# Attention, two mixtures and a router on one core: column maxima of k by halves, and the first batch's subtraction as matmuls into PSUM

## The chip, the cores and the metric

One NeuronCore of one Trainium2 chip runs the whole program. The engines are TensorE (PE; its weight loads are shown as PEld), VectorE (DVE), ScalarE (ACT), GpSimd (POOL) and SyncE (SP), which issues the DMAs here. Each engine runs its own list of instructions in order and waits on semaphores. The metric is the device time of one execution in microseconds; lower is better.

## The reference, cut to what matters

```python
q_s = exp(q - max(q, axis=-1));  q_s = q_s / (sum(q_s, axis=-1) + 1e-9)
k_s = exp(k - max(k, axis=2));   k_s = k_s / (sum(k_s, axis=2) + 1e-9)   # over the sequence
kv  = einsum('bhsd,bhse->bhde', k_s, v)
x   = einsum('bhsd,bhde->bhse', q_s, kv)      # 4 batches, 8 heads, 576 rows, 64 columns
x   = reshape(transpose(x), (2304, 512))
h   = maximum(x @ w_in, 0);  g = s * h * h + b;  x2 = g @ w_out          # 512 -> 2048 -> 512
out = one of 8 experts for each row of x2 (router, capacity 576)          # 512 -> 1024 -> 512
```

The maximum of k is taken for each batch, head and column over the 576 rows of the sequence, subtracted, and exponentiated. All inputs are float32.

## The kernel before

The program has four parts that overlap: linear attention, the dense layer (`h_unit`, `x2_unit`), the router, and the experts. Tokens go in nine groups of 256. Attention works by batch and by pair of heads: for batch b and pair j, `load_k` and `load_v` bring k and v, and a chain follows.

- `k_max` (L352) takes the maximum over the rows that lie in one partition, with one VectorE reduce. Batch 0 holds 96 partitions of 6 rows and both heads (96x768 in, 96x128 out), the other batches 128 partitions of 5 rows. Its result is in one of two buffers (tag `rt`).
- `k_T` (L359) transposes that on TensorE, `k_cm` (L366) reduces the transposed block on VectorE to one column `cm` (two buffers in pool `sm`).
- `k_bc` (L372) makes a matmul of `cm`, broadcast, with the identity, so that each partition has the maxima in a PSUM bank; `k_sub` (L377) subtracts it from k in place on VectorE, or on GpSimd after a copy by ScalarE for the pairs in `PAR["kpool"]`; `k_exp` (L388) is one ScalarE exponential in place.
- `k_kv` (L397) multiplies with v and a column of ones, `k_rec` and `k_blk` divide and write the block `kvb`.

For q there are `q_max`, `q_sub` (GpSimd), `q_exp`, `q_sum`, `q_norm` (GpSimd), the transposes `q_T`, `q_Te`, then `x1_mm` with `kvb`, and `x1_hi`, `x1_lo`, which split x into two parts (tiles x1h and x1l). Groups 0 and 1 come first, both of batch 0.

The weights of the dense layer arrive as 32 blocks of 512 KB and are converted by `cv_abs` (ScalarE), `cv_low`, `cv_sign`, `cv_join` (VectorE), `cv_hi` (ScalarE) and `cv_lo` (VectorE). `cv_sign` (L202) is done by VectorE for the blocks in `PAR["bv"]`, else by ScalarE. Sixteen-bit views (`half`) pick the sign bits.

A dense unit is 24 matmuls (L548 to L550) of a block of 256 tokens, one for each product of parts; it needs x1h and x1l of its group and the converted weight blocks. The first unit therefore waits for the whole chain of batch 0. Before it, `warm` matmuls on the identity fill gaps that the planner expects on TensorE.

What sets the order: every step has a slot, a shift in `PAR["d"]` (with `_0` for the early steps) is added, and `arrange` (L1503) places the steps engine by engine with a table of durations, of buffers and of dependences in `parts`. The engines then run exactly that order. The banks of batch 0's chain come from the four buffers `x2` of pool `ps_x`. `parts` doesn't list the buffers of `cm`.

Of the kernel before, what the change touches and what calls it, by code (L numbers as in the profile page):

```python
# [23 lines left out]


@with_exitstack
def kernel(ctx, tc, q, k, v, w_in, w_out, s_in, b_in, w_gate, w1, w2, cap, out, dbg=None):
    nc = tc.nc
    B, H, S, D = q.shape
# [4 lines left out]
    P = 128  # L34
# [6 lines left out]
    KR = S // P  # L41
# [104 lines left out]
    def at_slot(s, f, *a):  # L146
        plan.setdefault(s, []).append((f, a))
# [203 lines left out]

    def k_max(b, j):  # L352
        t = kt[b, j]
        p = P if b else P0
        m = at.tile([P, 2, D], F32, tag="rt", name="m1", bufs=2)
        nc.vector.tensor_reduce(out=m[:p], in_=t[:p].rearrange("p h r d -> p h d r"), axis=AX.X, op=ALU.max)
        kx[b, j] = m[:p]

    def k_T(b, j):  # L359
        m2 = kx[b, j]  # L360
        ps = aux(b, [P, P], "psk")
        p = m2.shape[0]
        nc.tensor.transpose(ps[:, :p], m2.rearrange("p h d -> p (h d)"), ident[:p, :p])
# [914 lines left out]
    def parts(f, a):  # L1278
# [18 lines left out]
        elif f in (k_max, k_T, k_cm, k_bc, k_sub, k_exp, k_kv, k_rec, k_blk):  # L1297
            k = b, j = a
            bank, kt_, vt_ = ("x2", f"wi{12 + j}", f"wo{12 + j}") if b == 0 else ("a", "k", "v")
            work, after, takes, gives = {  # L1300
                k_max: ([("DVE", 0.75 if b else 0.85)], [(load_k, *k)], ["rt"], []),
                k_T: ([("PE", 0.12)], [(k_max, *k)], [bank], [((k_max, *k), "rt")]),
                k_cm: ([("DVE", 0.29)], [(k_T, *k)], [], [((k_T, *k), bank)]),
                k_bc: ([("PE", 0.25)], [(k_cm, *k)], [bank], []),
                k_sub: (
                    [("ACT", 0.28), ("POOL", 1.75)] if k in PAR["kpool"] else [("DVE", 0.81 if b else 0.93)],
                    [(k_bc, *k)], ["bc"] if k in PAR["kpool"] else [], [((k_bc, *k), bank), (key, "bc")],
                ),
                k_exp: ([("ACT", 0.74 if b else 0.87)], [(k_sub, *k)], [], []),
                k_kv: (  # L1310
                    [("PE", 0.88 if b else 1.6)], [(k_exp, *k), (load_v, *k)], [bank], [((load_k, *k), kt_), ((load_v, *k), vt_)]
                ),
# [37 lines left out]
        elif f in (cv_abs, cv_low, cv_sign, cv_join, cv_hi, cv_lo):  # L1350
# [391 lines left out]
```

## Time and profile before

| | us |
|---|---|
| median of three runs | 562.85 (561.86 to 563.61) |
| the profiled execution, whole | 563.43 |
| its span, first to last instruction | 561.7 |
| TensorE busy | 536.7 (96%) |
| VectorE busy | 329.9 (59%) |
| ScalarE busy | 234.8 (42%) |
| GpSimd busy | 141.3 (25%) |

Times in the views are in us from the start of the span. A table by stage gives, for each stretch, its length and the busy time of PE, PEld, DVE, ACT and POOL with the number of instructions, then the granted clock of TensorE as a share of full speed, the mean busy share of the DMA engines and GB/s. A timeline row gives start, length, engine, line, operation, output and input tiles, and in brackets the idle time before it with what ended it; xN merges N instructions that follow each other, and a float32 matmul shows as two records. A row by form gives the count, the busy time in all and the mean in ns of one, then the idle time before the group. Line numbers are those of the kernel before. "SPq" is the queue that SyncE issues DMAs to.

### The profile page before, as it was taken

The page shows a single profiled execution, that of the slowest core. Times are in us where ns is not written, and L with a number is a line of the kernel's source. Part 1 is how long each engine was busy: PE and PEld are TensorE (multiplying, and loading weights), DVE is VectorE, ACT ScalarE, POOL GpSimd, SP SyncE. Part 2 cuts the span into 40 slices and gives each one's busy share as a digit, 9 for nine tenths or more (in the row PEclk, how much of TensorE's full clock was granted, in tenths as well). Part 3 has the DMA queues.
Part 4 walks back from the last instruction along what each step waited for, and adds up shares of the span by engine and source line. Part 5 has one row for each costly group of instructions (what it writes and reads, how often), then busy time and mean ns, then how long its engine had stood idle before and what let it go on. Part 6 is the DMA issues. An engine that isn't in the chain of part 4 may idle for free. (4 is left out here: it accounts for less than half of the span.)

```text
span 561.7 us, 10739 instructions
## 1 busy us (share of the span) xinstructions
PE 536.7 (96%) x4087; PEld 482.0 (86%) x4087; DVE 329.9 (59%) x743; ACT 234.8 (42%) x425; POOL 141.3 (25%) x198
## 2 busy tenths in 40 slices
PE   8889999999999999999999999999999899999993
PEld 7779998988988888999998899999888887899762
DVE  5999899996596678452646145473633576073010
ACT  2688868854533434332323323222342345162110
POOL 4240012212465455211131033320014116210111
PEclk9999999999999999999999999999999999999998
DMA  8988901044541322010010201006737029523000
GB/s 238 380 265 301 371 1 46 2 126 115 157 132 46 83 69 81 1 39 20 20 39 1 57 2 25 17 2 189 227 97 222 13 58 376 169 78 113 39 25 29
DMA packets 83332, 59.96 MB, mean 107 GB/s; under 512 B 40191, under 2 KB 75647, under 8 KB 83264
## 3 DMA queue, kind: packets, MB, share of 16 engines
q1 hardware_dynamic: 81104, 54.08, 31.7%
q0 software_dynamic: 2160, 5.01, 2.7%
q8 instruction: 39, 0.64, 0.5%
q14 instruction: 29, 0.24, 0.1%
HBM read 46.64 MB, written 12.51 MB: 105 GB/s over the span
## 5 line engine op out<-in xcount | busy, mean ns | idle before, releaser
L548 PE MATMUL psh<-x1h,wi 128*128 128x256 f32 x576 | 169.1, 294 | 1.3 <-PEq L652 0.4
L549 PE MATMUL psh<-x1l,wi 128*128 128x256 f32 x576 | 163.7, 284 | 1.5 <-DVE x1l L526 1.5
L550 PE MATMUL psh<-x1h,wi 128*128 128x256 f32 x576 | 163.6, 284 | 0.0
L548 PEld LDWEIGHTS psh<-x1h,wi 128*128 128x128 f32 x576 | 111.1, 193 | 5.7 <-issue 3.6
L549 PEld LDWEIGHTS psh<-x1l,wi 128*128 128x128 f32 x576 | 111.0, 193 | 2.6 <-DVE x1l L526 1.8
L550 PEld LDWEIGHTS psh<-x1h,wi 128*128 128x128 f32 x576 | 110.8, 192 | 0.0
L570 ACT ACTIVATE rt<-psh 128x512 f32<-128x512 f32 x44 | 26.3, 598 | 67.1 <-PE psh L550 63.5
L578 DVE SCALAR_TENSOR_TENSOR rt<-rt,sb_s 128x512 f32<-128x512 f32 x44 | 38.0, 863 | 26.8 <-ACT rt L570 26.6
L614 PE MATMUL psx<-wo,gh 128*128 128x512 f32 x128 | 51.8, 405 | 0.0
L615 PE MATMUL psx<-wo,gh 128*128 128x512 f32 x128 | 50.1, 391 | 0.0
L616 PE MATMUL psx<-wo,gl 128*128 128x512 f32 x128 | 50.0, 390 | 0.0
L570 ACT ACTIVATE rg<-psh 128x512 f32<-128x512 f32 x28 | 16.5, 597 | 60.4 <-PE psh L550 45.4
L578 DVE SCALAR_TENSOR_TENSOR rg<-rg,sb_s 128x512 f32<-128x512 f32 x28 | 21.9, 786 | 28.1 <-ACT rg L570 28.0
L473 POOL TENSOR_TENSOR qt<-qt,qm 128x512 f32<-128x512 f32 x14 | 16.6, 1204 | 80.5 <-DVE qm L465 68.0
L252 POOL TENSOR_TENSOR wS<-wo 128x128 f32<-128x128 f32 x64 | 32.1, 532 | 17.1 <-DVE wT L259 15.7
L600 DVE SCALAR_TENSOR_TENSOR gl<-rt,sb_b,gh 128x512 fp32r<-128x512 f32 x32 | 28.2, 884 | 5.6 <-ACT gh L591 5.6
L386 POOL TENSOR_TENSOR kt<-kt,bc 128x640 f32<-128x640 f32 (+1 forms) x8 | 14.9, 1858 | 59.5 <-ACT bc L382 59.5
L616 PEld LDWEIGHTS psx<-wo,gl 128*128 128x128 f32 x128 | 24.0, 188 | 5.3
L614 PEld LDWEIGHTS psx<-wo,gh 128*128 128x128 f32 x128 | 24.3, 190 | 4.8 <-issue 0.6
L964 POOL DMA_INDIRECT out<-y,mp x11 | 10.6, 965 | 70.1 <-ACT y L963 52.9
L491 POOL TENSOR_TENSOR qt<-qt,qs 128x1024 f32<-128x1024 f32 x7 | 14.7, 2103 | 53.6 <-DVE qs L486 53.0
L591 ACT ACTIVATE gh<-rt,sb_b 128x512 fp32r<-128x512 f32 x32 | 23.0, 718 | 12.1 <-DVE rt L578 12.0
(228 smaller groups left out, 1134.1 us busy)
## 6 DMA issues: line engine op xcount, KB each, us to landing
ri<-in_moe_w_in SPq DMA_DIRECT2D x16, 512.0 KB, 6.3
ro<-in_moe_w_out SPq DMA_DIRECT2D x16, 512.0 KB, 8.7
raw<-in_moe_w SPq DMA_DIRECT2D x12, 512.0 KB, 5.8
raw<-in_moe_w SPq DMA_DIRECT2D x24, 256.0 KB, 5.7
out<-zero SPq DMA_DIRECT2D x9, 512.0 KB, 6.7
kt<-in_k SPq DMA_DIRECT2D x12, 256.0 KB, 2.8
vt<-in_v SPq DMA_DIRECT2D x24, 128.0 KB, 3.0
x2d<-zero SPq DMA_DIRECT2D x5, 512.0 KB
```

The lines of the kernel that those rows point to most:

```text
L252: nc.gpsimd.tensor_tensor(t[:, c], hi, lo, ALU.add)
L473: nc.gpsimd.tensor_tensor(qt[n][:, :, r], t[:, :, r], qx[n][:, :, r:r + 1].to_broadcast([P, H, D]), ALU.subtract)
L548: nc.tensor.matmul(ps, wt[:, 0, o], xh[:, c % 2], start=(c == 0), stop=False)
L549: nc.tensor.matmul(ps, wt[:, 0, o], xl[:, c % 2], start=False, stop=False)
L550: nc.tensor.matmul(ps, wt[:, 1, o], xh[:, c % 2], start=False, stop=(c == NC - 1))
L570: nc.scalar.activation(t, ps, AF.Relu)
L578: nc.vector.scalar_tensor_tensor(t, t, sb_s, t, op0=ALU.mult, op1=ALU.mult)
L591: nc.scalar.activation(gh, t, AF.Identity, bias=sb_b)
L600: nc.vector.scalar_tensor_tensor(gl, t, sb_b, gh.bitcast(F32), op0=ALU.add, op1=ALU.subtract)
L614: nc.tensor.matmul(ps, gh[:, i, o], wt[:, 0], start=(f == 0), stop=False)
L615: nc.tensor.matmul(ps, gh[:, i, o], wt[:, 1], start=False, stop=False)
L616: nc.tensor.matmul(ps, gl[:, i, o], wt[:, 0], start=False, stop=(f == NF - 1))
```

## The change

Four things are changed, and the table of shifts.

- `k_max` for batches 0 and 1 takes, with one tensor_tensor, the maximum of the first and the second half of a partition's rows (96x384 out for batch 0; for batch 1 128x256, and a second one folds the odd row in). `k_T` then transposes three blocks for batch 0 and two for batch 1 into one bank, and `k_cm` reduces 288 or 256 columns.
- For batch 0 there is no `k_sub`. `k_bc` makes, for each head of a pair, two float32 matmuls of 384 columns into a bank: k times the identity, and `cm` broadcast times a negative identity `nid`. `k_exp` reads these banks, one ScalarE exponential of 96x384 for each head. `nid` is a new constant, written by ScalarE at the start.
- `cv_sign` on VectorE becomes a scalar_tensor_tensor on whole words with two tensor inputs, the two halves of the raw block.
- The table changes most shifts; `bv` goes from 19 to 15 blocks (i14, o1, o10, o5, o8 leave, o13 comes); pair (2, 1) leaves `kpool`. The planner's durations of the changed steps are adapted.

```diff
+            low, high = (raw[key][:, y].bitcast(U32) for y in range(2))
+            nc.vector.scalar_tensor_tensor(low, high, 0x80000000, low, op0=ALU.bitwise_and, op1=ALU.bitwise_or)
-            nc.vector.tensor_scalar(half[key][:, 1], half[key][:, 3], 0x8000, None, ALU.bitwise_and)
...
+        if b in WIDE:
+            p, n = (P, KR // 2) if b else (P0, R0 // 2)
+            m = at.tile([P, n, 2, D], F32, tag="rt", name="m3", bufs=2)
+            x = t[:p].rearrange("p h r d -> p r h d")
+            nc.vector.tensor_tensor(m[:p], x[:, 0:n], x[:, n:2 * n], ALU.max)
+            if b:
+                nc.vector.tensor_tensor(m[:, 0], m[:, 0], x[:, KR], ALU.max)
+            kx[b, j] = [m[:p, i].rearrange("p h d -> p (h d)") for i in range(n)]
+            return
...
+        ps = aux(b, [P, len(blocks), p], "psk")
+        for i, x in enumerate(blocks):
+            nc.tensor.transpose(ps[:, i], x, ident[:p, :p])
...
+        nc.vector.tensor_reduce(out=cm, in_=ps.rearrange("p i r -> p (i r)"), axis=AX.X, op=ALU.max)
...
+        if b == 0:
+            cm, t = kx[b, j], kt[b, j]
+            kx[b, j] = [aux(b, [P, R0, D], "psd") for h in range(2)]
+            for h, ps in enumerate(kx[b, j]):
+                neg = nid[:, h * D:(h + 1) * D].unsqueeze(1).to_broadcast([P, R0, D])
+                nc.tensor.matmul(ps[:P0], ident[:P0, :P0], t[:P0, h], start=True, stop=False)
+                nc.tensor.matmul(ps[:P0], cm.to_broadcast([P, P0]), neg, start=False, stop=True)
+            return
...
+        if b == 0:
+            for h, ps in enumerate(kx.pop((b, j))):
+                nc.scalar.activation(t[:P0, h], ps[:P0], AF.Exp)
+            return
...
-        at_slot(z + 4, k_sub, 0, j)
...
-PAR = {'d': {'w_asm': -9.6, 'h_sq': -5.9, 'x2_kept': 22.5, 'r_keep': -1.9,
+PAR = {'d': {'w_asm': -9.6, 'h_sq': -5.4, 'x2_kept': 22.3, 'r_keep': -1.9,
```

The order moves in three places that matter later in this text. On VectorE, at the start of the program, before the change (m is a maximum, cm a column maximum, qs a q sum, rec the reciprocal for kvb; in brackets the engines or DMA queues whose semaphore is waited for):

```order
L356 TENSOR_REDUCE m_148<-kt 96x128 [waits DMAHW2_49]
L356 TENSOR_REDUCE m_153<-kt 96x128 [waits DMAHW3_49]
L356 TENSOR_REDUCE m_198<-kt 96x128 [waits DMAHW4_49,PE_49]
L356 TENSOR_REDUCE m_210<-kt 96x128 [waits DMAHW5_49,PE_49]
L369 TENSOR_REDUCE cm<-psk 128x1 x2
L369 TENSOR_REDUCE cm<-psk 128x1 [waits PE_49] x2
L386 TENSOR_TENSOR kt<-kt,psb 96x768 x2
L386 TENSOR_TENSOR kt<-kt,psb 96x768 [waits PE_49]
L484 TENSOR_REDUCE qs<-qe 128x16 [waits Activation_49]
```

On VectorE at the same place after the change (line numbers are those of the changed kernel; L199, L208 and L223 are cv_low, cv_sign and cv_join):

```order
L362 TENSOR_TENSOR m_195<-kt 96x384 [waits DMAHW4_49,DVE_49,PE_49]
L362 TENSOR_TENSOR m_207<-kt 96x384 [waits DMAHW5_49,DVE_49,PE_49]
L382 TENSOR_REDUCE cm<-psk 128x1 x2
L382 TENSOR_REDUCE cm<-psk 128x1 [waits DVE_49,PE_49] x2
L508 TENSOR_REDUCE qs<-qe 128x16 [waits Activation_49]
L509 TENSOR_SCALAR qs<-qs 128x16 [waits DVE_49]
L510 RECIPROCAL qs<-qs 128x16 [waits DVE_49]
L199 TENSOR_SCALAR ri_214<-ri_214 128x512 [waits DMAHW2_49]
L208 SCALAR_TENSOR_TENSOR ri_214<-ri_214 128x512 [waits DVE_49]
L223 SCALAR_TENSOR_TENSOR cT<-cT,ri_214 128x512 [waits DVE_49,Activation_49]
```

The subtraction is gone, and the q sum follows the column maxima; the third and fourth column maximum wait for TensorE in both orders, for the matmuls that read the first and the second cm.

On TensorE, from the fourth maximum's transpose on, before the change (psb is the broadcast, pskv the product with v):

```order
L363 MATMUL psk<-ident,m_210 128x96 [waits DVE_49]
L374 MATMUL psb<-ident,cm 128x128 [waits DVE_49] x4
L1601 MATMUL warm<-ident 128x128 x8
L405 MATMUL pskv<-vt,kt 64x128 [waits DMAHW2_49,DMAHW6_49,Activation_49,Pool_49]
L405 MATMUL pskv<-vt,kt 64x128 x11
```

On TensorE at the same place after the change (psd is the difference in PSUM, psq a transpose of q):

```order
L376 MATMUL psk<-ident,m_207 128x96 [waits DVE_49]
L376 MATMUL psk<-ident,m_207 128x96 x2
L1626 MATMUL warm<-ident 128x128 x2
L391 MATMUL psd<-kt,ident 96x384 [waits DMAHW2_49,DVE_49,PE_49]
L392 MATMUL psd<-nid,cm 96x384 [waits Activation_49]
L391 MATMUL psd<-kt,ident 96x384 [waits DVE_49,PE_49]
L392 MATMUL psd<-nid,cm 96x384
L391 MATMUL psd<-kt,ident 96x384 [waits DMAHW3_49,Activation_49]
L392 MATMUL psd<-nid,cm 96x384
L391 MATMUL psd<-kt,ident 96x384 [waits Activation_49]
L392 MATMUL psd<-nid,cm 96x384
L429 MATMUL pskv<-vt,kt 64x128 [waits DMAHW6_49,DVE_49,Pool_49]
```

Four short broadcasts gave way to the long pairs, of which the second pair of heads waits for ScalarE; pairs 2 and 3 (not shown) come after the products and q transposes of pairs 0 and 1.

On ScalarE, from the exponentials of q on, before the change:

```order
L479 ACTIVATE qe<-qe 128x1024 [waits Pool_49] x2
L382 ACTIVATE bc<-psb 128x128 [waits PE_49]
L390 ACTIVATE kt<-kt 96x768 [waits DMAHW2_49,DVE_49]
L390 ACTIVATE kt<-kt 96x768 [waits DMAHW3_49,DVE_49]
L390 ACTIVATE kt<-kt 96x768 [waits DMAHW5_49,DVE_49]
L390 ACTIVATE kt<-kt 96x768 [waits DMAHW4_49,Pool_49]
L215 ACTIVATE cT<-ri_204 128x512 [waits DMAHW2_49]
```

On ScalarE at the same place after the change (L218 is cv_abs, L230 cv_hi, L412 k_exp):

```order
L503 ACTIVATE qe<-qe 128x1024 [waits Pool_49] x2
L218 ACTIVATE cT<-ri_214 128x512 [waits DMAHW2_49]
L412 ACTIVATE kt<-psd 96x384 [waits DVE_49,PE_49]
L412 ACTIVATE kt<-psd 96x384 [waits PE_49]
L230 ACTIVATE wi_285<-cT 128x512 [waits DVE_49]
L412 ACTIVATE kt<-psd 96x384 [waits DMAHW3_49,PE_49]
L412 ACTIVATE kt<-psd 96x384 [waits PE_49]
L218 ACTIVATE cT<-ri_225 128x512 [waits DMAHW6_49]
```

The first cv_abs, which waits for a weight block's DMA, moved ahead of the exponentials of k, and a cv_hi, which waits for VectorE, stands between those of pair 0 and pair 1.

## Rows read from the trace of the kernel before

**Rows 1.** Busy time by stage; columns as told above.
```profile
16.70:20.50 3.80, 3.80 (x62) 3.68 (x62) 3.69 (x9) 3.75 (x7) 1.97 (x2) 1.00 1.08 405
...
40.50:44.10 3.60, 3.60 (x17) 3.60 (x18) 3.60 (x7) 1.89 (x4) 0.00 (x0) 0.53 1.03 370
44.10:48.00 3.90, 3.90 (x34) 3.90 (x34) 3.58 (x8) 3.13 (x7) 0.00 (x0) 0.99 1.04 388
...
80.00:100.00 20.00, 20.00 (x144) 17.96 (x143) 19.82 (x32) 15.40 (x26) 6.10 (x4) 1.00 0.14 32
```

**Rows 2.** Waits of TensorE from 280 to 480 us: total, times, longest.
```profile
PE psx L641 <- ACT gg L635: 1.1, 1, 1.1
```

**Rows 3.** Timeline of VectorE up to the fourth x1l.
```profile
7.71 2.92 DVE L356 TENSOR_REDUCE m<-kt 96x128 f32<-96x768 f32 x2
11.30 2.87 DVE L356 TENSOR_REDUCE m<-kt 96x128 f32<-96x768 f32 x2 [0.68 <-PE psk L363]
...
14.92 0.48 DVE L369 TENSOR_REDUCE cm<-psk 128x1 f32<-128x96 f32 x2 [0.42 <-PE psb L374]
...
17.91 1.21 DVE L484 TENSOR_REDUCE qs<-qe 128x16 f32<-128x1024 f32 x1
...
19.75 2.46 DVE L197 TENSOR_SCALAR ri<-ri 128x512 uint32<-128x512 uint32 x2
...
29.80 1.79 DVE L220 SCALAR_TENSOR_TENSOR cT<-cT,ro 128x512 int32<-128x512 int32 x1
...
39.75 0.69 DVE L526 TENSOR_TENSOR x1l<-psx,x1h 128x512 fp32r<-128x512 f32 x1
```

**Rows 4.** Timeline of TensorE up to the first unit.
```profile
9.79 1.39 PE L1601 MATMUL warm<-ident 128*128 128x128 f32 x11
...
17.66 5.46 PE L405 MATMUL pskv<-vt,kt 96*64 96x128 f32 x96
...
30.45 1.03 PE L512 MATMUL psx<-qT,kvb 128*128 128x256 f32 x4
31.31 0.60 PE L499 MATMUL psq<-ident,qe 128*128 128x128 f32 x4
...
40.50 0.40 PE L549 MATMUL psh<-x1l,wi 128*128 128x256 f32 x1 [1.47 <-DVE x1l L526]
```

**Rows 5.** Timeline of ScalarE: the exponentials of k, and the first Relu.
```profile
16.29 3.31 ACT L390 ACTIVATE kt<-kt 96x768 f32<-96x768 f32 x4 [0.26 <-DMA ri<-in_moe_w_in]
...
44.33 0.60 ACT L570 ACTIVATE rt<-psh 128x512 f32<-128x512 f32 x1 [0.22 <-PE psh L550]
```

**Rows 6.** Groups by form: count, busy us, mean ns of one.
```profile
L220 DVE SCALAR_TENSOR_TENSOR cT<-cT,ri 128x512 int32<-128x512 int32 x16 | 11.0, 695 | 0.0
...
L356 DVE TENSOR_REDUCE m<-kt 128x128 f32<-128x640 f32 x12 | 15.7, 1305 | 7.6 <-DMA kt<-in_k 7.6
...
L369 DVE TENSOR_REDUCE cm<-psk 128x1 f32<-128x128 f32 x12 | 3.4, 284 | 2.5 <-PE psk L363 2.3
...
L369 DVE TENSOR_REDUCE cm<-psk 128x1 f32<-128x96 f32 x4 | 0.9, 252 | 0.4 <-PE psb L374 0.4
...
L386 DVE TENSOR_TENSOR kt<-kt,psb 96x768 f32<-96x768 f32 x3 | 2.7, 943 | 0.0
...
L520 ACT ACTIVATE x1h<-psx 128x512 fp32r<-128x512 f32 x18 | 10.8, 599 | 10.8 <-PE psx L512 10.8
...
L526 DVE TENSOR_TENSOR x1l<-psx,x1h 128x512 fp32r<-128x512 f32 x18 | 12.3, 686 | 10.9 <-ACT x1h L520 10.7
```

**Rows 7.** Issues of the DMA queue: the first block of w_in, and the entry behind it.
```profile
7.70 0.39 SPq L186 DMA_DIRECT2D ri<-in_moe_w_in  x1
...
16.74 0.37 SPq L186 DMA_DIRECT2D ri<-in_moe_w_in  x1
```

**Rows 8.** Timeline of GpSimd: q_sub, and the second q_norm.
```profile
7.81 4.06 POOL L473 TENSOR_TENSOR qe<-qt,qm 128x512 f32<-128x512 f32 x4 [5.29 <-DVE qm L465]
...
28.89 2.15 POOL L491 TENSOR_TENSOR qe<-qe,qs 128x1024 f32<-128x1024 f32 x1 [6.97 <-DVE qs L486]
```

More of the change, by code (lines that the diff above doesn't have):

```diff
@@ new lines @@
+PAR = {'d': {'w_asm': -9.6, 'h_sq': -5.4, 'x2_kept': 22.3, 'r_keep': -1.9, 'r_T': -11.1, 'k_blk': 6.4, 'gemm1_ahead': 20.4, 'w_x': 10.9, 'q_max': -24.0, 'load_v': -11.2, 'q_sum': 13.7, 'r_Te': -3.2, 'r_pos': 10.4, 'load_k': -17.2, 'conv1': 9.4, 'r_back': -18.7, 'load_q': -8.1, 'h_aff': -96.7, 'load_raw2': -11.3, 'h_relu': -16.6, 'q_norm': -0.4, 'x1_lo': -21.9, 'x1_mm': -8.8, 'w_sum': -12.6, 'r_lt': 14.9, 'h_hi': -0.3, 'r_scat': 41.0, 'cv_low': 9.8, 'cv_sign': 14.4, 'zero_x2d': 9.3, 'zero_out': 120.8, 'cv_hi': -4.9, 'x1_hi': 11.7, 'cv_abs': 15.2, 'w_add': 20.9, 'w_shift': -21.3, 'r_hot': -15.3, 'load_w': 8.6, 'k_cm': -14.5, 'x2_evac': 18.0, 'w_tr': -6.8, 'g_load': 28.1, 'h_lo': 0.3, 'w_mm': -2.4, 'k_bc': -3.8, 'r_logit': -14.8, 'q_sub': 8.0, 'k_rec': -13.0, 'cv_lo': -19.2, 'q_Te': -1.7, 'k_sub': -12.6, 'r_pre': 6.7, 'q_exp': -13.2, 'cv_join': 0.7, 'k_max': 17.9, 'k_exp': -1.3, 'q_T': -7.9, 'k_kv': -8.1, 'k_T': -6.1, 'r_fuse': 4.5, 'x1_lo_0': 14.7, 'x1_mm_0': 27.4, 'q_sub_0': -33.3, 'k_bc_0': 15.6, 'k_sub_0': -4.3, 'k_T_0': -46.2, 'k_kv_0': 3.5, 'cv_hi_0': 18.6, 'q_max_0': -81.3, 'load_k_0': -30.9, 'q_Te_0': 19.1, 'k_exp_0': -11.5, 'q_exp_0': -31.2, 'k_rec_0': 31.1, 'x1_hi_0': -19.8, 'q_norm_0': -15.6, 'cv_join_0': -9.0, 'cv_low_0': 5.3, 'cv_sign_0': -15.3, 'q_sum_0': 8.7, 'cv_lo_0': -0.2, 'cv_abs_0': 0.1, 'load_v_0': -17.7, 'k_blk_0': -18.2, 'k_max_0': -71.0, 'q_T_0': 11.7, 'load_w_0': -4.5, 'k_cm_0': -2.9, 'load_q_0': -143.1}, 'bv': ['i0', 'i1', 'i10', 'i11', 'i15', 'i3', 'i4', 'i7', 'i8', 'o0', 'o11', 'o13', 'o14', 'o3', 'o9'], 'ahead': 4, 'win': 0, 'slack': 0.0, 'zk': -20, 'zq0': -12, 'zq1': -24, 'ci0': -2, 'ci1': 0, 'co0': 0, 'co1': -4, 'zl': 93, 'soft0': 0, 'soft1': 0, 'kpool': ((0, 2), (1, 0), (1, 1), (1, 2), (1, 3), (2, 3), (3, 0)), 'k1': [10, 2], 'k2': [-71, 3], 'k3': [-14, 2]}
@@ L76 @@
     ident = const.tile([P, P], F32, name="ident")
+    nid = const.tile([P, P], F32, name="nid")
     tri = const.tile([P, P], BF16, name="tri")
@@ L97, in consts_first @@
         make_identity(nc, ident)
+        nc.scalar.activation(nid, ident, AF.Copy, scale=-1.0)
         for j in range(NPAIR):
@@ L309 @@
     P0 = 96
+    WIDE = (0, 1)
     R0 = S // P0
@@ L353, in k_max @@
         t = kt[b, j]
-        p = P if b else P0
+        if b in WIDE:
[7 more added lines that the diff above has]
+            return
         m = at.tile([P, 2, D], F32, tag="rt", name="m1", bufs=2)
-        nc.vector.tensor_reduce(out=m[:p], in_=t[:p].rearrange("p h r d -> p h d r"), axis=AX.X, op=ALU.max)
-        kx[b, j] = m[:p]
+        nc.vector.tensor_reduce(out=m, in_=t.rearrange("p h r d -> p h d r"), axis=AX.X, op=ALU.max)
+        kx[b, j] = [m.rearrange("p h d -> p (h d)")]
     def k_T(b, j):
[L360 to L363, printed above, removed]
+        blocks = kx[b, j]
+        p = blocks[0].shape[0]
+        ps = aux(b, [P, len(blocks), p], "psk")
+        for i, x in enumerate(blocks):
+            nc.tensor.transpose(ps[:, i], x, ident[:p, :p])
         kx[b, j] = ps
@@ L1354, in parts @@
                 cv_low: ([("DVE", 0.43)], [(load_w, *k)], [], []),
-                cv_sign: ([("DVE", 0.43) if by_vector(k) else ("ACT", 1.38)], [(cv_low, k)], [], []),
+                cv_sign: ([("DVE", 0.7) if by_vector(k) else ("ACT", 1.38)], [(cv_low, k)], [], []),
                 cv_join: ([("DVE", 0.68)], [(cv_abs, k), (cv_sign, k)], [], [((load_w, *k), f"w{w_}{c}")]),
```

21 lines of the change are left out of this document (10 added, 11 removed).

## The prediction, made before the changed kernel ran

> **What bounds the kernel now.** I read the busy table by stage first. From 44 us on TensorE never waits for long: it does 34 matmuls in the 3.9 us after 44.1 and is busy 20.00 of 20.00 us between 80 and 100 [rows 1]. What moves the end is therefore the moment at which the dense layer's matmuls start to flow, plus a few waits of about 1 us far later, of which one is shown [rows 2]. A late start is paid one for one, since no later stretch has idle TensorE time to give back.
>
> Before that start, VectorE sets the pace. It is busy 3.69 of 3.80 us from 16.7 [rows 1] and has no gap after that, and its timeline shows the chain: maxima of k from 7.71, column maxima at about 14 to 15.3, the first q sum at 17.91, and the fourth x1l, 39.75 + 0.69 = 40.44 [rows 3]. TensorE waits for that x1l and resumes at 40.50 [rows 4]. It then runs at half clock (granted 0.53 from 40.5 to 44.1, 17 matmuls in 3.60 us against 34 in 3.90 after it [rows 1]), and the first unit's 24 matmuls end at about 44.3, where ScalarE's first Relu starts [rows 5]. The half clock costs 17 x (3.60/17 - 3.90/34) = 1.65 us.
>
> So I walk the new order up to the fourth x1l and the end of the first unit, and compare with 40.44 and 44.3.
>
> **Maxima by halves.** Four reduces of 1.46 us each (2.92 for two [rows 3]) become four tensor_tensor of 96x384. The rows for 512 and 768 elements of such an operation, 0.686 and 0.943 us [rows 6], give about 1 ns an element, so 0.56 us each. But the transposes of the first max stand behind the warm-up matmuls, which ran until 11.0 before (9.79 + 1.39 is the end modelled for the last [rows 4]; 30 instead of 31 end at about 10.8), and the third max needs the first one's buffer. So the third starts at about 11.1 instead of 11.30 and the fourth ends near 12.3 instead of 11.30 + 2.87 = 14.17 [rows 3]: 1.9 us won, not the 3.6 us of the work. The column maxima now read 288 elements instead of 96: 0.252 us for 96 and 0.284 for 128 [rows 6] give 0.45, so the first two are ready at about 12.7 and 13.1. The fourth pair's transposes and two warm-up matmuls end at about 13.0.
>
> **The subtraction on TensorE.** VectorE loses three tensor_tensor of 0.943 us [rows 6] and GpSimd one; TensorE gets 16 matmuls of 384 columns. Two f32 matmuls of 256 columns took 31.31 - 30.45 = 0.86 us, 0.43 each [rows 4]; 384 columns cost 0.645, so a pair's four cost 2.58 us at full clock.
>
> The column max (tile cm) has two buffers. Before, the third k_cm waited for one 128-column matmul of the first pair, and VectorE lost 0.42 us [rows 3]. Now it waits for all four matmuls of pair 0 (13.0 + 2.6 = 15.6 us), and the fourth k_cm for all four of pair 1. These need the banks that pair 0's exp empties. In ScalarE's new order the exp stands behind the first cv_abs, which needs the first block of w_in. That block's DMA, issued at 7.70, lands when the queue entry that reuses its semaphore goes out, at 16.74 [rows 7]; before, that cv_abs stood behind the four exp, which end at 16.29 + 3.31 = 19.60 [rows 5]. Its place among the DMAs doesn't change. So: cv_abs ends at about 17.3 (0.55 us of ScalarE), exp of the first half at 17.8 (384 elements: between half of 3.31/4 and the 0.599 us of 512 elements out of PSUM [rows 5, 6]; I take 0.5), pair 1's matmuls from 17.85 to 20.4, and the fourth k_cm from 20.5 to 20.95.
>
> Queued behind that k_cm on VectorE stand the q sums, all weight conversion and all x1l. VectorE idles from 13.1 to 15.7 and from 16.1 to 20.5, 7 us in all. The first q sum starts at 20.95 instead of 17.91 [rows 3]: **3.0 us later**, although VectorE has 2.8 us of subtraction and 3.6 us of maxima less to do.
>
> **From the q sum to the fourth x1l.** Before, this took 40.44 - 17.91 = 22.5 us. The list is the same but for one cv_sign and one cv_join more, about 0.69 us each by the similar row [rows 6], and a cv_sign form that is that row's shape too. That gives 22.5 + 1.5 = 24.0, and the fourth x1l ends at 45.0 at the least. It isn't that good, for ScalarE's order ties itself to VectorE: the first cv_hi stands ahead of pair 1's exp and waits for the join of the first block, and two q_norm of GpSimd fall into cv_low and cv_sign. A join next to the q_norm at 28.89 took 1.79 us, two cv_low took 2.46 us [rows 3, 8]. My walk: q sum and reciprocal until 22.6, join of block 0 at 25.5 to 26.2 behind the q_norm, exp of pair 1 at 26.8 to 27.7, its k_kv (5.46/4 us [rows 4]) until 29.1, pair 2's and 3's matmuls 29.6 to 34.8, second q_norm holding VectorE from 30.7 to 32.5, exp of pair 3 until 36.8, k_kv until 38.2, x1 products from 39.9, idle VectorE from 40.5 to 41.8 for a cv_hi, fourth x1l until **47.2**. The two ends are 45.0 and 47.2, 4.6 and 6.8 us behind 40.44.
>
> **The first unit.** After the fourth x1l 18 matmuls remain. At full clock (3.90/34 = 0.115 us each [rows 1]) they take 2.1 us, at half clock as before 3.8. So the first unit ends between 47.1 and 51.0, against 44.3: +2.8 to +6.7. I take +5.0: the walk's 47.2 with full clock (+5.0), or the floor with half clock (+4.5), come to nearly the same.
>
> **The rest.** Batch 1's maxima by halves save, by 1 ns an element, about 0.6 us each of 1.305 us [rows 6] on VectorE and add a transpose each on TensorE; 15 instead of 19 sign passes are left on VectorE; one subtraction of batch 2 comes to VectorE. TensorE is full there (20.00 of 20.00 [rows 1]), so this is worth nothing to the end; without that cover it would be some 2 us. The order of TensorE after 200 us is as before, so I leave the late waits ([rows 2], 5 us in all) as they are, plus or minus 1.5 us. The profiled execution took 563.43 us for a span of 561.7; with +5.0 it would be 568.4. The median of the runs is 0.6 lower, so I forecast **567.9**.
>
> **The rivals.** (1) *VectorE's relief decides, faster.* If the fourth k_cm didn't wait, the q sum would start when the four column maxima end, 12.3 + 1.8 = 14.1 us, 3.8 earlier than 17.91; less the 1.5 of added work the first unit ends 2.3 us earlier: 560.5. It decides from the point where the fourth k_cm starts before about 16.0. For it speaks that VectorE has no idle time before [rows 1]; against it the 0.42 us wait for a single matmul and the landing at 16.74 [rows 3, 7]. Chance 0.12.
> Two of the old maxima, reduces, took 2.92 us beside q_sub and the next two 2.87 us, mostly after it [rows 3, 8]. The Trainium skill, page SBUF — State Buffer, section Who interferes with whom, states that a VectorE instruction with two SBUF inputs is shut out while a GpSimd instruction reads SBUF, and that tensor_reduce never is, with which the trace agrees; the new max has two SBUF inputs and falls beside the q_sub. No row here shows that form beside q_sub. By the rule two maxima would wait up to one q_sub each, about 1 us, and rival 1 would shrink to about 562.5; the forecast stays, as the landing at 16.74 covers it.
> (2) *The stalls don't come back.* The two q_norm miss cv_low and cv_sign, which gives back about 1.1 + 1.6 us by the rows of 1.79 and 2.46 us [rows 3] against 0.69 and two 0.42: 568.4 - 5.0 + 2.3 for the profile, 565.2 for the median. Chance 0.15.
> (3) *The clock falls earlier too.* TensorE is idle from 21.8 to 25.0 and from 25.5 to 27.7 in my walk, longer than the idle stretch of 1.5 us before the half clock at 40.5 [rows 1, 4]. A half-clock stretch there doubles four of the new matmuls, 2.6 us more, and the first unit's end gets the 1.65 as well: about 571.5. Chance 0.13.
> That the change isn't in the program can be left out: the order of instructions shows it.
>
> **How the numbers follow.** Forecast +2.8 to +6.7: 0.60; rivals 0.12, 0.15, 0.13. About 0.3% (1.7 us) is what a measurement of this kernel tells from no change. Slower: 0.60 + 0.13 and half of rival 2, 0.80. Same: the other half of rival 2 and a third of rival 1, 0.12. Faster: 0.08. The range leaves out rival 1 and the upper end of rival 3: 563.5 to 572.
>
> **What would show it.** In the profile of the changed kernel: two idle stretches of VectorE ahead of the third and fourth k_cm that TensorE ends, 2.5 and 4.4 us; the first q sum at about 21; the first exp behind a cv_abs that a DMA releases at 16.7; the new matmuls at 0.64 us apart; the fourth x1l at 45 to 47; first Relu at 47 to 51; and from there the same spacing as before to the end. A fourth k_cm before 17 us, a first Relu before 44 or a stretch after 100 us that is shorter by over 2 us would show me wrong.

## The result and the profile after

The changed kernel took 568.26 us in the median of four executions (567.9 to 570.17), the kernel before 563.23 (561.86 to 563.63); the ratio is 1.0101 with a 95% interval of 1.0071 to 1.013. The forecast was 567.9. Executions far off the rest, such as one of 665.38 us at a granted clock of 0.75 with the four buffers below, are left out of the ratios.

| | before | after |
|---|---|---|
| the profiled execution, whole | 563.43 | 567.94 |
| its span | 561.7 | 566.1 |
| TensorE busy | 536.7 | 539.8 |
| VectorE busy | 329.9 | 322.8 |
| first q sum starts | 17.91 [rows 3] | 20.43 |
| fourth x1l ends | 40.44 [rows 3] | 47.97 |
| first Relu starts | 44.33 [rows 5] | 50.54 |

VectorE has 7.1 us less to do and the kernel is 5.0 us slower. Line numbers of the changed kernel are higher than before, by 2 or 3 at the weights' conversion and by 24 from the q steps on. VectorE's timeline of the changed kernel, the places that answer to [rows 3]:

```profile
11.81 1.64 DVE L362 TENSOR_TENSOR m<-kt 96x384 f32<-96x384 f32 x2 [2.31 <-PE psk L376]
13.38 0.81 DVE L382 TENSOR_REDUCE cm<-psk 128x1 f32<-128x288 f32 x2
17.07 0.46 DVE L382 TENSOR_REDUCE cm<-psk 128x1 f32<-128x288 f32 x1 [2.88 <-PE psd L392]
20.05 0.46 DVE L382 TENSOR_REDUCE cm<-psk 128x1 f32<-128x288 f32 x1 [2.53 <-PE psd L392]
20.43 1.21 DVE L508 TENSOR_REDUCE qs<-qe 128x16 f32<-128x1024 f32 x1
...
22.45 2.28 DVE L208 SCALAR_TENSOR_TENSOR ri<-ri 128x512 uint32<-128x512 uint32 x1
...
30.12 1.53 DVE L199 TENSOR_SCALAR ro<-ro 128x512 uint32<-128x512 uint32 x1
...
42.48 0.69 DVE L234 TENSOR_TENSOR wi<-cT,wi 128x512 fp32r<-128x512 f32 x1 [1.48 <-ACT wi L230]
...
47.29 0.68 DVE L550 TENSOR_TENSOR x1l<-psx,x1h 128x512 fp32r<-128x512 f32 x1
```

The brackets hold the story: the third and the fourth column maximum wait 2.88 and 2.53 us, both for the last of a pair's subtraction matmuls (psd, L392). At this operation VectorE lost 0.42 us before [rows 3]; now it loses 5.4 us. TensorE, in answer to [rows 4]:

```profile
14.28 0.81 PE L391 MATMUL psd<-kt,ident 96*96 96x384 f32 x2
14.93 0.81 PE L392 MATMUL psd<-nid,cm 128*96 128x384 f32 x2
...
17.19 0.89 PE L391 MATMUL psd<-kt,ident 96*96 96x384 f32 x2 [0.16 <-ACT kt L412]
...
19.21 0.81 PE L392 MATMUL psd<-nid,cm 128*96 128x384 f32 x2
19.95 1.53 PE L429 MATMUL pskv<-vt,kt 96*64 96x128 f32 x24
...
26.61 3.20 PE L429 MATMUL pskv<-vt,kt 96*64 96x128 f32 x24 [1.72 <-ACT kt L412]
...
48.03 0.38 PE L573 MATMUL psh<-x1l,wi 128*128 128x256 f32 x1 [0.23 <-DVE x1l L550]
```

From 14.28 to 14.93 is one f32 matmul of 384 columns: 0.65 us. The second pair (17.19) is released by the exp of the first (kt, L412), and that stands on ScalarE behind a step that a DMA releases, in answer to [rows 5]:

```profile
16.09 0.67 ACT L218 ACTIVATE cT<-ri 128x512 f32<-128x512 f32 x1 [2.43 <-DMA ri<-in_moe_w_in]
16.67 0.89 ACT L412 ACTIVATE kt<-psd 96x384 f32<-96x384 f32 x2
25.55 0.63 ACT L230 ACTIVATE wi<-cT 128x512 fp32r<-128x512 f32 x1 [8.00 <-DVE cT L223]
26.09 0.84 ACT L412 ACTIVATE kt<-psd 96x384 f32<-96x384 f32 x2
...
50.54 0.59 ACT L594 ACTIVATE rt<-psh 128x512 f32<-128x512 f32 x1
```

The table by stage, for the stretch at low clock before the first unit, and for the 3.9 us behind that unit (before: 44.10 to 48.00 in [rows 1]):

```profile
25.00:31.00 6.00, 4.39 (x29) 3.90 (x30) 5.59 (x13) 3.98 (x9) 1.79 (x1) 0.50 1.07 395
...
50.50:54.40 3.90, 3.90 (x35) 3.90 (x34) 3.77 (x8) 3.53 (x8) 0.00 (x0) 1.00 1.04 350
```

The half clock now lies at 25 to 31 us, where TensorE is busy 4.39 of 6.00 us, and not in the first unit. Behind the first unit TensorE is as full as before. The first Relu is 6.21 us late; the span is 4.4 us longer. What lies between shows on ScalarE late in the program, at the same two steps of before and of after. Before:

```profile
443.11 1.09 ACT L836 ACTIVATE xB<-psg 128x512 fp32r<-128x512 f32 x2
...
451.08 0.44 ACT L868 ACTIVATE hB<-psy 128x320 fp32r<-128x320 f32 x1 [1.77 <-PE psy L867]
```

After:

```profile
449.39 1.08 ACT L860 ACTIVATE xB<-psg 128x512 fp32r<-128x512 f32 x2
...
455.83 0.44 ACT L892 ACTIVATE hB<-psy 128x320 fp32r<-128x320 f32 x1 [0.80 <-PE psy L891]
```

The distance is 6.28 us at the first step, so since 50 us it had only been carried along, and 4.75 us at the second. Between them the kernel before ran at half clock and the changed one didn't. The table by stage of before, that stretch:

```profile
446.90:450.30 3.40, 3.40 (x15) 3.40 (x14) 1.41 (x6) 0.95 (x2) 0.00 (x0) 0.50 0.00 0
440.00:446.90 6.90, 5.11 (x38) 4.33 (x37) 4.04 (x18) 2.23 (x5) 1.94 (x2) 1.00 0.03 5
```

And of after, the same work 6.3 us later:

```profile
453.20:456.60 3.40, 3.40 (x25) 3.40 (x24) 1.86 (x8) 1.73 (x4) 0.00 (x0) 1.00 0.02 5
446.30:453.20 6.90, 5.11 (x38) 4.33 (x37) 4.03 (x18) 2.24 (x5) 1.94 (x2) 1.00 0.02 5
```

So the loss of the change is made in the first 51 us, and in these two profiles the clock took 1.53 us of it back.

### The profile page after: what moved, and what is told of

Read it like the earlier page. It is cut to its first block, busy times and chain, and to the rows that moved or that the text cites. A ratio compares the mean times of both kernels' runs of the same rounds, so it can differ in the third digit from the quotient of the medians.

```text
span 566.1 us, 10662 instructions
## 1 busy us (share of the span) xinstructions
PE 539.8 (95%) x4055; PEld 478.9 (85%) x4055; DVE 322.8 (57%) x741; ACT 239.4 (42%) x432; POOL 138.1 (24%) x196
## 3 DMA queue, kind: packets, MB, share of 16 engines
q0 software_dynamic: 2160, 5.01, 2.8%
## 5 line engine op out<-in xcount | busy, mean ns | idle before, releaser
L602 DVE SCALAR_TENSOR_TENSOR rg<-rg,sb_s 128x512 f32<-128x512 f32 x28 | 22.1, 793 | 26.8 <-ACT rg L594 26.6
L638 PEld LDWEIGHTS psx<-wo,gh 128*128 128x128 f32 x128 | 24.1, 188 | 5.2 <-issue 1.0
L639 PEld LDWEIGHTS psx<-wo,gh 128*128 128x128 f32 x128 | 24.1, 189 | 4.0
L624 DVE SCALAR_TENSOR_TENSOR gl<-rt,sb_b,gh 128x512 fp32r<-128x512 f32 x32 | 24.7, 773 | 4.3 <-ACT gh L615 4.3
```

Of the source, the lines that this page charges most:

```text
L602: nc.vector.scalar_tensor_tensor(t, t, sb_s, t, op0=ALU.mult, op1=ALU.mult)
L624: nc.vector.scalar_tensor_tensor(gl, t, sb_b, gh.bitcast(F32), op0=ALU.add, op1=ALU.subtract)
L638: nc.tensor.matmul(ps, gh[:, i, o], wt[:, 0], start=(f == 0), stop=False)
L639: nc.tensor.matmul(ps, gh[:, i, o], wt[:, 1], start=False, stop=False)
```

## The experiments

**Four buffers for the column maximum.** The theory: the loss hangs on the two buffers of cm, which the planner's table of buffers doesn't know.

```
-        cm = sm.tile([P, 1], F32, tag="cm", name="cm")
+        cm = sm.tile([P, 1], F32, tag="cm", name="cm", bufs=4)
```

> The changed kernel, its order untouched, with four buffers instead of two for the column maximum cm. My theory (VectorE is held ahead of the third and fourth column maximum by the pair's subtraction matmuls): the two idle stretches of 2.88 and 2.53 us go, the first q sum starts at about 14.7 us instead of 20.43 and everything that hangs on it shifts by 5 to 6 us: fourth x1l at 42 to 43 instead of 47.97, first Relu at 44.5 to 46 instead of 50.54, time 562 to 564 us, that is 4.5 to 6 us below the changed kernel. Rival A (the loss is GpSimd shutting out VectorE's new two-input operations, the sign pass of 2.28 us and the maxima of 0.88): these stay, the gain is under 1.5 us, 567 or more. Rival B (ScalarE's order, cv_hi ahead of the second pair's exp, sets the pace, whatever VectorE does): first Relu falls by less than 3 us, time about 565 to 567.

Measured: 563.25 us, ratio to the kernel before 1.0009 (0.9988 to 1.003). Against the changed kernel's 1.0101 this one number gives back 0.92%, 5.2 us. The edit holds for the columns of all batches. The timeline is that of a single further execution.

> The changed kernel with four cm buffers once more, for a profile at full TensorE clock (the first one ran at a granted 0.75 from end to end). My theory: four column maxima in a row, first q sum at 14.5 to 15.5 us, and then VectorE waits for what was hidden, the first weight block's landing (16.1 to 18.5), ahead of the first cv_low; first Relu 44.5 to 46.5, time 562 to 564.5. If ScalarE's order (second pair's exp behind the first cv_hi) costs anything here, VectorE shows idle time ahead of a k_rec that TensorE ends, 1 us or more in sum.

Measured: 563.53 us; first Relu 44.68, fourth x1l until 42.11. VectorE's timeline of that run:

```profile
13.81 1.54 DVE L382 TENSOR_REDUCE cm<-psk 128x1 f32<-128x288 f32 x4
15.27 1.20 DVE L508 TENSOR_REDUCE qs<-qe 128x16 f32<-128x1024 f32 x1
...
17.75 1.55 DVE L199 TENSOR_SCALAR ri<-ri 128x512 uint32<-128x512 uint32 x1 [0.78 <-DMA ri<-in_moe_w_in]
...
36.62 0.69 DVE L234 TENSOR_TENSOR wi<-cT,wi 128x512 fp32r<-128x512 f32 x1 [1.54 <-ACT wi L230]
...
41.43 0.68 DVE L550 TENSOR_TENSOR x1l<-psx,x1h 128x512 fp32r<-128x512 f32 x1
```

And ScalarE's:

```profile
21.39 0.84 ACT L412 ACTIVATE kt<-psd 96x384 f32<-96x384 f32 x2
...
44.68 0.59 ACT L594 ACTIVATE rt<-psh 128x512 f32<-128x512 f32 x1
...
443.51 1.09 ACT L860 ACTIVATE xB<-psg 128x512 fp32r<-128x512 f32 x2
```

Four maxima in a row and the first q sum at 15.27 instead of 20.43. No k_rec waits for TensorE. At the first Relu this run is 5.86 us ahead of the changed kernel, and still 5.88 us at 443.51, ahead of the late stretch. The cause of the loss is settled: the buffer, not GpSimd (rival A) and not ScalarE's order (rival B). But the q sum is 2.64 us ahead of the kernel before and the fourth x1l 1.67 us behind it, so the new order spends 4.3 us more between the two. Of these, 2.3 us are the two idle stretches in brackets, where [rows 3] had none; one more sign pass and one more join are some 1.3 us, an estimate from two of 0.69 us each; the rest isn't assigned.

**ScalarE's order alone, and with the buffers.** Two buffers as in the changed kernel, the exp of both pairs moved forward:

```
...
+        put_ahead(seq, (k_exp, (0, 1)), (cv_hi, (("i", 0),)))
+        put_ahead(seq, (k_exp, (0, 0)), (cv_abs, (("i", 0),)))
...
```

> The changed kernel with two buffers as it is, and only two instructions moved on ScalarE: the first pair's exp ahead of the first cv_abs, the second pair's exp ahead of the first cv_hi. My theory: the fourth column maximum still waits for the second pair's matmuls and starts at most 0.4 us earlier (19.65 to 20.05), but VectorE loses its later idle stretches (0.88 us at 38.0, 1.48 at 42.5), since the second pair's exp starts at about 20 us instead of 26.1: first Relu 47.5 to 49 instead of 50.54, 1.5 to 3 us gained, time 565 to 567. Rival B (ScalarE's order sets everything): over 4 us gained, under 564. Rival A (GpSimd's shut-outs): under 1 us gained.

Measured: 566.86 us, ratio 1.0057 (1.0035 to 1.0079), some 2.5 us below the changed kernel by the ratios, whose intervals just overlap; first Relu 48.89, 1.65 us earlier. VectorE still waits, ahead of the fourth maximum only 0.4 us less:

```profile
16.87 0.46 DVE L382 TENSOR_REDUCE cm<-psk 128x1 f32<-128x288 f32 x1 [2.89 <-PE psd L392]
19.46 0.46 DVE L382 TENSOR_REDUCE cm<-psk 128x1 f32<-128x288 f32 x1 [2.13 <-PE psd L392]
...
40.81 0.69 DVE L234 TENSOR_TENSOR wi<-cT,wi 128x512 fp32r<-128x512 f32 x1 [1.55 <-ACT wi L230]
```

So ScalarE's order is a second, smaller cost of the changed kernel. Of the two later idle stretches that were to go, the one of 0.88 us went; that of 1.48 us ahead of a cv_lo stayed, at 1.55, and the run with four buffers has it too. With the four buffers and the second pair's exp ahead of the cv_hi:

> The changed kernel with four cm buffers and the second pair's exp ahead of the first cv_hi. My theory: the two gains add, 4.5 to 6 and 1.5 to 2.5 us; first Relu at 42.5 to 44, time 560 to 562 us, below the kernel before (563.2). If the gains share one cause, no more than the larger of the two single edits: 562.5 to 564.

Measured: 563.41 us, ratio 1.0002 (0.9983 to 1.0021); first Relu 44.40 against 44.68. The gains don't add. With four buffers the second pair's exp starts at 21.39 anyway instead of 26.09, since the join that the cv_hi waits for comes as soon as VectorE is free: both waits hung on the same late VectorE. What VectorE waited for in this run was new:

```profile
18.54 0.43 DVE L199 TENSOR_SCALAR ri<-ri 128x512 uint32<-128x512 uint32 x1 [2.40 <-DMA ri<-in_moe_w_in]
```

**The first weight block's DMA ahead of the loads of v.** On top of that kernel, with both exp forward:

```
...
+        z = next(x for x in seq if x[0] is load_w and x[1] == ("i", 0))
+        seq.remove(z)
+        seq.insert(next(y for y, x in enumerate(seq) if x[0] is load_v), z)
...
```

> The changed kernel with four cm buffers, both exp moved ahead on ScalarE, and the first weight block's DMA issued ahead of the four v loads instead of behind them. If the landing of that block (18.5 us in the run before with 2.40 us of idle VectorE) has become the bound: the idle stretch ahead of the first cv_low goes, the first exp starts at about 15 instead of 19.1, first Relu 1 to 2.5 us earlier than 44.4, time 560.5 to 562.5 and less spread between runs. Rival (GpSimd's q_norm, which now lies beside cv_low and cv_sign, holds VectorE instead): cv_low and cv_sign of the first block take 2 us or more in sum beyond their 1.1, first Relu gains under 0.7 us, time 562.5 to 563.5.

Measured: 563.47 us, ratio 1.0028 (1.0005 to 1.0051); first Relu 44.26, 0.14 us gained. The rival holds in its time and its Relu; what cv_low and cv_sign of the first block lost is 1.5 us, not the 2 that it asked for. VectorE's timeline:

```profile
16.55 2.28 DVE L208 SCALAR_TENSOR_TENSOR ri<-ri 128x512 uint32<-128x512 uint32 x1
...
19.93 0.43 DVE L199 TENSOR_SCALAR ri<-ri 128x512 uint32<-128x512 uint32 x1 [0.31 <-DMA ri<-in_moe_w_in]
...
25.16 1.18 DVE L199 TENSOR_SCALAR ro<-ro 128x512 uint32<-128x512 uint32 x1 [0.77 <-DMA ro<-in_moe_w_out]
```

The 2.40 us of waiting became 1.6 us of a sign pass held beside q_norm (2.28 against 0.69) and two later landings.

**The parts alone, in the old order.** Each was put into the kernel before, its order as it was. First the maxima by halves of batch 0:

```
...
+            m = at.tile([P, n, 2, D], F32, tag="rt", name="m3", bufs=2)
...
+            nc.vector.tensor_tensor(m[:p], x[:, 0:n], x[:, n:2 * n], ALU.max)
...
```

> The kernel before, its order untouched, with the maxima by halves and the transposed blocks for batch 0 alone. By my prediction's term: the third maximum starts at about 11.1 and the fourth ends near 12.5 instead of 14.17, the four column maxima cost 0.2 us more each, the first q sum starts about 1.0 us earlier than 17.91, and this carries to the first Relu (43.3 instead of 44.33) and to the end: 562.2, a ratio of 0.998. Rival 1 of the prediction (VectorE's relief is worth its whole work, 3.6 us less 0.8): 560.4. Rival: hidden, no change, if the weights' landing at 16.7 or ScalarE's exp sets the next step.

Measured: 561.69 us, ratio 0.9983 (0.9957 to 1.0009). Once more, with more executions:

> The kernel before in its old order with the maxima by halves of batch 0 alone, once more in five rounds, since three left its ratio at 0.9983 with an interval that held 1. If the 0.3 us that the first q sum gained there (17.60 against 17.91) are all of it: 0.9985 to 1.0, not to be told from no change. If my term of 1.0 us holds: 0.998 with an interval below 1.

Measured: 561.82 us, ratio 0.9996 (0.9976 to 1.0015): no change, and the first q sum at 17.60 against 17.91 in the first of the two. Why not 1.0 us, the timelines of the two show, the first run's:

```profile
7.89 5.37 DVE L359 TENSOR_TENSOR m<-kt 96x384 f32<-96x384 f32 x4
```

And the second run's:

```profile
11.10 2.12 DVE L359 TENSOR_TENSOR m<-kt 96x384 f32<-96x384 f32 x2 [1.53 <-PE psk L371]
```

In the first run four maxima that take 0.55 us where nothing disturbs them took about 1.33 us from start to start, with no idle time ahead of any, all beside GpSimd's q_sub. In the second the third one waited 1.53 us for transposes, and the last two took 2.12 us. The fourth ended at 13.26 and at 13.22, in both runs some 0.4 us behind the last q_sub (12.84 and 12.81), where 12.5 was expected. The four q_sub took 5.01 and 4.93 us there, against 4.06 beside the reduces [rows 8], and two reduces took 2.92 in the same place [rows 3]. The Trainium skill (page SBUF — State Buffer, section Who interferes with whom) has the rule: a VectorE instruction with two SBUF inputs contends with a GpSimd instruction that reads SBUF, a reduce never does. The trace agrees.

The subtraction on TensorE alone, with four cm buffers (k_sub of batch 0 left empty):

> The kernel before in its old order with the subtraction on TensorE alone (four cm buffers, maxima by the old reduce, old sign pass). By my price of 0.645 us a matmul the sixteen run from about 14.4 to 24.8 in one row, ahead of every k_kv in that order; the first k_rec on VectorE, 19.53 before, comes at about 27, and all weight conversion stands behind it: first Relu 50 to 52, time 569 to 571. Rival (VectorE's 2.8 us less work decides): first q sum at 15.1 and first Relu at 42, time under 562.

Measured: 573.37 us in a single execution, first Relu 51.51. VectorE's timeline:

```profile
16.20 0.25 DVE L502 RECIPROCAL qs<-qs 128x16 f32<-128x16 f32 x1
28.27 0.16 DVE L429 TENSOR_SCALAR rec<-pskv 128x1 f32<-128x1 f32 x1 [11.82 <-PE pskv L421]
```

TensorE's, from the first subtraction matmul to what follows the last:

```profile
14.39 0.89 PE L380 MATMUL psd<-kt,ident 96*96 96x384 f32 x2
...
24.82 1.95 PE L1617 MATMUL warm<-ident 128*128 128x128 f32 x16
```

The price per matmul held, sixteen in 10.43 us, and the old order cannot bear it: all sixteen stand ahead of the products, and VectorE is idle for 11.82 us until the first of these is done. The first Relu lies where it was expected; the time is 2.4 us above the range, and that is late: the distance to the kernel before was 5.84 us at 420 us and 9.94 at 492, with a granted clock of 0.55 from 470 to 477 in this run.

The two-input sign pass alone:

> The kernel before in its old order with the two-input sign pass alone. My term: 0.69 us each with 0.61 from start to start, against 0.53 to 0.60 for the old form; some seven of them lie ahead of the fourth x1l, so that ends 0.3 to 0.6 us later, time 563.0 to 564, not to be told from no change. Rival A (the two-input form is shut out by GpSimd where the old one isn't): over 1.5 us later, 564.5 or more.

Measured: 562.84 us, ratio 1.0023 (1.0001 to 1.0045), at the edge of what can be told from no change. From the first q sum (17.04) to the end of the fourth x1l (39.71) it took 22.67 us, against 22.53 before. So in the old order the form is as good as neutral where the chain runs, and rival A has no support there, though by the interval alone up to 2.5 us are possible. Beside a q_norm the same pass took 2.28 us, in the changed kernel and in the run with the first weight block's DMA ahead.

**Another order of the x1 products.** Four buffers and the second pair's exp forward, then the tail rewritten: products of group 0 first, both x1l ahead of the conversion of later blocks, warm-up matmuls there taken out.

```
...
+        tail = [(k_rec, 0, 3), (cv_join, i2), (x1_mm, 0, 0), (q_Te, 0, 1), (k_blk, 0, 3), (x1_hi, 0, 0), (x1_lo, 0, 0), (x1_mm, 0, 1)]
+        tail += [(cv_hi, i2), (x1_hi, 0, 1), (x1_lo, 0, 1), (cv_lo, i2)]
+        tail += [(f, 1, hf) for hf in range(2) for f in (x1_mm, x1_hi, x1_lo)]
...
```

> The changed kernel with four cm buffers, the second pair's exp ahead of the first cv_hi, and the tail before the dense layer in another order: the products x1 of group 0 first, both groups' x1l ahead of the conversion of blocks that only later units read, no warm-up matmuls in between. If the late start is now a matter of the order of x1 alone (VectorE does four conversion steps between the x1l, ScalarE's qT stands behind other work): the fourth x1l ends at about 38.5 to 39.5 instead of 41.8, first Relu at 41 to 42.5 instead of 44.4, time 559.5 to 561.5, below the kernel before. Rival (the work only moves: VectorE or ScalarE owe the same conversion a few units later and TensorE waits there): first Relu early, but a new TensorE wait of 1 us or more between 44 and 60, time 562 to 563.5.

Measured: 564.57 us, ratio 1.0044 (1.0016 to 1.0072). TensorE started the first unit at 39.40 and ran it through, then:

```profile
47.30 0.39 PE L572 MATMUL psh<-x1h,wi 128*128 128x256 f32 x1 [1.81 <-ACT rt L594]
```

The Relu of the first unit stood behind conversion work on ScalarE until 46.65, and TensorE waited for it to get a bank. So the rival's wait came, but the Relu wasn't early and the time is 1.1 us above the rival's range. With the Relu of the first two units moved ahead of that work:

> The kernel of the run before (four cm buffers, x1 of group 0 first), and in addition the Relu of the first two units moved ahead of the conversion steps on ScalarE that stood before them. If what cost that kernel its gain was ScalarE's conversion work ahead of the first Relu (46.65 us although the first unit's matmuls ended near 42.3, and a TensorE wait of 1.81 us at 47.3 for the bank): first Relu at 42.5 to 44, no such wait, and from unit 2 on everything 2 to 2.3 us earlier than there; time 560.5 to 562.5, at or below the kernel before (562.8). Rival (the conversions that are pushed back are late themselves): TensorE waits 1 us or more between 46 and 60 for an x2 operand or a weight block, time 563 to 565.

Measured: 563.99 us, ratio 1.0042 (1.002 to 1.0064); first Relu 42.91, 1.4 us earlier than before, and then:

```profile
49.51 0.50 PE L638 MATMUL psx<-wo,gh 128*128 128x512 f32 x1 [1.58 <-ACT gh L615]
```

Here the rival held, in its wait and its time. I read the two waits so: before 50 us ScalarE and VectorE owe a sum of conversion work, and TensorE waits for it at one place or another. No run takes conversion work away, so this is argued and not shown. No version here beats the kernel before clearly.

Not run by themselves: the new table of shifts, the sign passes that moved to ScalarE, pair (2, 1), and the maxima of batch 1. With four buffers all of the change together can't be told from no change (1.0009).

**Warm-up matmuls in TensorE's last wait, kernel before.**

```
...
+        seq.insert(seq.index((h_unit, (0,))), (warm, (16,)))
...
```

> The kernel before with sixteen warm-up matmuls more ahead of the first unit, in the time in which TensorE waits for the fourth x1l. They change no data and lie in a wait of 1.47 us, of which some 0.4 us would be left. If the half clock after that wait (40.5 to 44.1 us, 1.65 us lost) comes from TensorE having stood idle: no stretch at half clock there, median 561 to 562 us. If it falls by itself in some executions whatever precedes it: no difference to the kernel before, 562.5 to 563.3 us.

Measured: 565.93 us, ratio 1.0063 (1.0036 to 1.009): outside both expectations. I had given the sixteen some 1.1 us of the wait of 1.47; they took some 3.5, so the first unit started behind them, at 40.92, and its Relu at 44.16 was only 0.17 earlier. The warm-up matmuls, and the table by stage late in the run:

```profile
37.43 3.73 PE L1601 MATMUL warm<-ident 128*128 128x128 f32 x32
...
464.00:468.00 4.00, 3.86 (x10) 3.09 (x11) 3.22 (x4) 3.23 (x6) 3.54 (x4) 0.57 1.07 403
```

There was no half clock at 40 to 44, as the first answer has it; but the sign-pass run had none there either, with its wait left empty (last section), so this doesn't show what brings it. In this run half clock lay at 464 to 468 us instead of 446 to 450, and the distance to the kernel before went from 1.65 us ahead at 451 to 1.27 behind at 492. Why the later place costs more is open. The profiled execution took 564.55 us, 1.4 less than the median of the ten; what the others lost beyond it isn't shown.

## Why the prediction held, step by step

**The wait that decides: right.** Two idle stretches ahead of the third and fourth k_cm, ended by TensorE, were forecast at 2.5 and 4.4 us and measured 2.88 and 2.53, so the second was 1.9 us too long, as the third column maximum came later and the fourth earlier than in the walk. The run with four buffers takes them away and the 5 us with them. Rival 1 assumed that the fourth k_cm doesn't wait. That run is its case, and even there its 560.5 was too low, since idle time and cv_low passes of up to 1.86 us beside a q_norm took the place of the wait.

**The price of a subtraction matmul: right**, 0.65 us against 0.645.

**The maxima: wrong in size, without effect.** "0.56 us each" holds only undisturbed. Beside q_sub they took up to 1.17 us here and 1.33 in the old order. The two last took 1.64 us instead of 1.12, and they started at 11.81 instead of 11.1, behind transposes that the warm-up matmuls held until 11.36. So the fourth ended at 13.45 instead of 12.3, and the first psd started at 14.28 instead of 13.0. The rule that the prediction weighed there and left out of its sum, from the Trainium skill (page SBUF — State Buffer, section Who interferes with whom), pointed the right way for the first part.

**The landing of the first weight block: 0.65 us off the other way.** It came at 16.09 instead of 16.74, so the first exp ran at 16.67 and the fourth k_cm at 20.05 instead of 20.5. The first q sum shows this error and not that of the maxima, 20.43 against 20.95: pair 0's matmuls ended at about 17.0, just before its exp freed the bank, so their lateness was covered.

**The walk to the fourth x1l: right within 0.8 us, in part by luck.** From the q sum to the x1l it gave 26.3 us and 27.5 were measured; the early q sum hid 0.5 of that. The second pair's exp was forecast at 26.8 and came at 26.09, the first step held beside a q_norm was 2.28 us long and the second 1.53 (rival 2 had them free), idle time for a cv_hi late in the walk at 1.3 us and measured 1.48. The end was 47.97 against 47.2 for the walk and 45.0 for the floor.

**The clock: half of rival 3 came.** TensorE's idle time behind the first k_kv (2.75 and 1.72 us) was followed by half clock: the second k_kv took 3.20 us against 1.53 for the first at full clock. But then the first unit ran at full clock, which rival 3 had not assumed. (Its sum, 567.9 + 2.6 + 1.65, comes to 572.15 and not to 571.5.) The first Relu started at 50.54, inside 47.1 to 51.0, though 1.2 us above the +5.0 that I took: 0.8 came from the walk, and the Relu stood behind a conversion step on ScalarE while the unit's last matmul had started at 50.04. Of the 18 matmuls that the prediction lets remain, 17 are in the row [rows 1].

**"The rest" was mis-sized.** I left the part after 100 us as it was, plus or minus 1.5; it gave back 1.8. There the half clock of the kernel before (446.9 to 450.3) didn't come back, which gave 1.53 us. So the forecast of 567.9 for 568.26 is closer than its steps: +6.2 at the first Relu, -1.5 from the clock, a few tenths more at the end, +4.4 in the span, where +5.0 was forecast. And the 0.6 us taken off for the median of the runs was not there: here the median is 0.3 above the profiled execution.

## What to carry to other kernels

When an operation is moved to another engine, list its operands' buffers and ask which of them is now held longer: here a column of 128 numbers with two buffers, held until the last of four long matmuls instead of one short one, made 5 us of the time, although VectorE had 7.1 us less to do. A planner that doesn't know a buffer will place instructions behind a wait that it can't see. And a milestone such as the first unit measures only its own chain: bringing it forward by reordering was paid back at a later wait in both tries.

## What the runs showed of the hardware

The same idle time isn't always followed by half clock. TensorE's work in the 6.9 us ahead of the late stretch was equal in the kernel before, in the changed kernel and in that with four buffers (5.11 us busy, 38 matmul records). The first fell to 0.50 and the second stayed at 1.00, as shown above. The third, which differs from the second in the buffers of cm alone, fell:

```profile
440.40:447.30 6.90, 5.11 (x38) 4.33 (x37) 4.04 (x18) 2.24 (x5) 1.94 (x2) 1.00 0.02 5
447.30:450.70 3.40, 3.40 (x15) 3.40 (x15) 1.46 (x6) 0.96 (x2) 0.00 (x0) 0.51 0.00 0
```

Ahead of the first unit, the sign-pass run had this wait, as long as that of before [rows 4], and no low clock behind it:

```profile
39.76 0.39 PE L550 MATMUL psh<-x1l,wi 128*128 128x256 f32 x1 [1.50 <-DVE x1l L527]
```

The Trainium skill (page TensorE: Matmul & The Clock Gate, Part 1) says of the climb to full clock that it varies from run to run; of the fall these rows show the same. The kernel before alone went from 559.36 us at a mean granted clock of 0.994 to 564.42 at 0.989 within one set of nineteen executions. A comparison of two single profiles therefore carries some 1.5 us a stretch that belong to neither kernel, and more where the stretch lies late: the distance moved by 2.9 us in the run with warm-up matmuls.

The landing of the first weight block, 16.09 us in one run and 18.54 in another with the same order on the DMA queue (issued at 7.62 and at 8.53), was the other thing that moved from run to run.
